# The last sixteen attention groups scored and valued in couples, with the scheduler's durations refitted

## The chip, the cores and the metric

The kernel runs on one core of a Trainium2 chip. The metric is the device time of one execution in microseconds (us); less is better. A profile is one execution recorded by the hardware. PE is TensorE's matmul side (PEld its weight loads, which run beside the multiplications), DVE is VectorE, ACT ScalarE, POOL GpSimd, and SP is SyncE, whose queue issues the DMAs.

## What is computed

A windowed attention over 8 batches x 8 heads x 576 positions x 64 numbers, and a feed-forward layer with a softplus behind it, all in fp32:

```python
scores = scale * np.matmul(q, k.transpose(0, 1, 3, 2))
mask_plain = (rel >= 0) & (rel < window)                     # window 32, heads 0 to 3
mask_dil = (rel >= 0) & (rel < window * dilation) & (rel % dilation == 0)   # dilation 4, heads 4 to 7
...
attn = np.exp(scores)
attn = attn / (np.sum(attn, axis=-1, keepdims=True) + 1e-09)
return np.matmul(attn, v)                                    # becomes x, 4608 x 512
...
h = x @ w_in                                                 # 512 x 2048
g = np.maximum(h, 0.0) + np.log1p(np.exp(-np.abs(h)))
return g @ w_out                                             # 2048 x 512
```

## The kernel before

**Tiles.** The 4608 tokens are 9 chunks of 512. Each chunk has 4 pairs of heads, so there are 36 groups of attention, numbered n = 4 x chunk + pair; pairs 0 and 1 are plain, 2 and 3 dilated. The feed-forward products work on 128 x 512 tiles; each fp32 operand is split into a high and a low part, so a product is three multiplications (a step of two tiles is six). The last six chunks are taken as three doubles of two chunks, each computed with seven products of blocks in place of eight. There are 3168 multiplications of 128 x 512 in the program, before and after the change. Positions in the program are given below by their count: "B 1296" is the place behind 1296 of them.

**A group of attention.** PE visits it twice. The scores visit (32 small multiplications into the PSUM tile `sv_ps`; the trace counts 64 records) multiplies `k` and `q`. Then DVE adds the mask (`maximum`, L441) and takes the maximum (L452), ACT does eight exponentials (L463), DVE sums, divides and turns 32 x 32 squares (L475 to L503). SP sends the squares to a DRAM tile `turned` (`send_squares`) and brings them back in four DMAs as `pt` (`fetch_squares`, the task "bring"). The values visit (32 small multiplications, 64 records) multiplies `pt` and `v`, and ACT copies the result into x (L589, `x_full`). `sv_ps` is two banks of PSUM. The scores of group n and the values of group n-1 share it: scores in the left half of each bank, values in the right (`HALF`). In order, then, PE scores n, values n-1, scores n+1, and so on; the two can be one visit ("jointly") or two.

**What sets the order.** PE, DVE, ACT and SP each run their queue in program order. The opening is written out by hand; from group 12 on (`double`) a planner inside the program writes all queues: a list scheduler that advances a clock, with a `Task` for each operation (engine, cost in us, what it waits for) and `choose(t)` for what PE does next. `visits` is the list of attention visits; a scores visit is taken when `t >= spaced` and, unless its time is urgent, when the values can join it (`joins`), else a product is taken. Multiplications pass through `matmul` (L238) and DMAs through `load_dma` (L173), so all of them have one line in the profile. The costs are numbers like these (`attention` and `values_of`):

```python
s = scored[n] = Task(f"scores {n}", PE, 1.06, lambda: score_of(n), deps)
v = valued[n] = Task(f"values {n}", PE, 1.30, lambda: value_of(n), deps)
together[scored[n]] = Task(f"both {n}", PE, 2.10, both)
```

The feed-forward work around the visits has PE write `h_x` and `h_y` (a block's product x @ w_in) and `o_ps` (g @ w_out); ACT and DVE combine them (L1424, L1426), compute the softplus (`e`, L1437 to L1447), and split g (L1467, L1471). SP streams the weights `t<-w_o`, `t<-w_two` and the like through rotating tiles.

Of the kernel before, what the change touches and what calls it, by code (L numbers as in the profile page):

```python
# [24 lines left out]
P = 128  # L25
# [44 lines left out]
MARGIN = 0.4  # L70
VISIT_EVERY = 8.0
NEG = -1.0e9
DEPTH = 4
# [43 lines left out]
def tile_windowed_attention_softplus_ffn(  # L117
# [35 lines left out]
    identb = consts[:, :P]  # L153
    ident = const.tile([P, P], F32, name="ident")
    slots, at = [], {0: 0, 1: 0, 2: 0}
# [144 lines left out]
    x_full, blocks = {}, {}  # L300

    def x_half(c, k):
        if (c, k) not in x_full:
            tag = "x_" + ("abcd" if c == FIRST else "cdab")[2 * ((c - FIRST - 1) % 2) * (c > FIRST) + k]
            x_full[c, k] = const.tile([P, 2, CH], F32, name="x_full", tag=tag)
        return x_full[c, k]
# [57 lines left out]
    class Group:  # L364
# [7 lines left out]
        def __init__(self, c, pr):  # L372
            self.c, self.pr, self.dil = c, pr, pr >= NPR // 2
            self.n, self.scaled_by, self.beside = c * NPR + pr, None, None
            self.own, self.masked = c == 0, c < 2
            self.places = PLACES[self.n] if self.n < len(PLACES) else "aaa"

        def load_k(self, engine=None):
            kw = DKW if self.dil else PKW
            self.k = scratch([P, kw], "k", self.c, self.pr)  # L380
            src = kdl[self.c, self.pr - 2] if self.dil else kpl[self.c, self.pr]
            load_dma(engine, out=self.k, in_=src)

        def load_q(self):
            self.q = scratch([P, CH], "q", self.c, self.pr)
            load_dma(out=self.q, in_=qp[self.c, self.pr])
# [5 lines left out]
        def load_v(self):  # L392
            self.v = scratch([P, NB, 2, D], "v", self.c, self.pr)
# [5 lines left out]
        def score(self, shared=None):  # L399

            self.banks, self.scored = shared or two_banks(
                "s_ps", {"a": None, "h": "hh", "o": ("o1", "o2")}[self.places[0]]
            )
            for t in range(NS):
                for g in range(NG):
                    for r in range(2):
                        rows = slice(r * D, (r + 1) * D)
                        q0, k0 = first_of(self.dil, t, g)
                        matmul(
                            out=self.banks[r][g * BLK : (g + 1) * BLK, t * WKEYS : (t + 1) * WKEYS],  # L410
                            lhsT=self.q[rows, q0 : q0 + BLK],
                            rhs=self.k[rows, k0 : k0 + WKEYS],
                            start=not self.masked or t == 0,
                            stop=not self.masked,
                        )
# [9 lines left out]
        def maximum(self):  # L425
            self.s = s = scratch([P, 2 * SW], "s", self.c, self.pr)
            self.blocks = s.rearrange("p (t k) -> p t k", k=WKEYS)
# [72 lines left out]
        def turn_squares(self):  # L500

            squares = const.tile([P, NG, NS, SQ], F32, name="squares", tag="q1")
            pin(nc.vector.transpose(  # L503
# [8 lines left out]
        def fetch_squares(self):  # L512
            self.pt = scratch([P, NG, NS * SQ], "pt", self.c, self.pr)
            for c in range(NG):
# [20 lines left out]

        def weighted(self, shared=None, following=None):

            banks, src = shared or two_banks("a_ps", ("o1", "o2") if self.places[2] == "o" else None)
            if shared:
                banks, src = [b[:, HALF:] for b in banks], [b[:, :, HALF:] for b in src]  # L540
# [44 lines left out]
        def x_high(self):  # L585
            if self.c >= FIRST:
                self.x = x_half(self.c, self.pr // 2)[:, self.pr % 2], None, self.src
            for dh, _, src in self.x_parts():
                copied = nc.scalar.copy(out=dh, in_=src)  # L589
                pin(copied)  # L590
                if self.c >= FIRST and self.n + 1 < len(groups):
# [334 lines left out]
    def value_of(n):  # L926

        if n + 1 < len(groups):
# [102 lines left out]
    class Ring:  # L1031
# [7 lines left out]
        def take(self, until):  # L1039
            self.holders = self.holders[1:] + [until]  # L1040

    class Task:

# [14 lines left out]
        def open(self, t):  # L1058
            return (
                self.after <= t + 1e-9  # L1060
                and all(
                    d.over(t + LATENCY * (getattr(d, "engine", PE) == self.engine != PE)) for d in self.deps
                )
# [40 lines left out]
    def run(task, t, engine=PE):  # L1104
# [111 lines left out]

    last_sum, last_more = [None], [None]

    def sums_of(i, p, deps):

        over = {}
        takes = lambda what: [(a_ring, Later(lambda: over.get(what)))]
        rank = 4.0
# [59 lines left out]

    def loads(n):
        if n >= len(groups):
            return
        g = groups[n]
        loaded[n, "q"] = Task(f"q {n}", SP, 0.256, g.load_q, [scored[n - 1]], rank=0.9)
        loaded[n, "k"] = Task(f"k {n}", SP, 0.32, g.load_k, [scored[n - 1]], rank=0.9)
        if g.pr == 0:  # L1290
            masks_in[g.c] = Task(f"mask {g.c}", SP, 0.128, lambda: load_mask(g.c), [scaled_of[n - 1]], rank=0.9)

    def values_of(n):

        deps = [brought.get(n), loaded.get((n, "v")), scaled_of.get(n + 1), x_done.get(n - 1)]
        v = valued[n] = Task(f"values {n}", PE, 1.30, lambda: value_of(n), deps)
        if n + 1 < len(groups):
            loaded[n + 1, "v"] = Task(f"v {n + 1}", SP, 0.512, groups[n + 1].load_v, [v], rank=1.0)
# [4 lines left out]
    def attention(n):  # L1303

        soon[0] = SOONER
        if n == len(groups):
            values_of(n - 1)
            return
# [7 lines left out]
        loads(n + 1)  # L1316
        values_of(n - 1)
        for t in range(NB):
            last = Task(
# [3 lines left out]
        last = Task(f"divide {n}", DVE, 0.70, lambda: g.divide(nc.vector), [last], rank=0.3)  # L1323
        last = turned_of[n] = Task(f"turn {n}", DVE, 0.71, g.turn_squares, [last, sent_squares.get(n - 1)], rank=0.3)
        last = sent_squares[n] = Task(f"send {n}", SP, 0.256, g.send_squares, [last], rank=0.1)
        brought[n] = Task(f"bring {n}", SP, 0.5, g.fetch_squares, [last, valued[n - 1]], rank=0.1)

# [202 lines left out]
    for d in range(DOUBLES):  # L1530
        for p in range(NPAIR):
            for k, (x, weights, role, begins, to, temp) in enumerate(steps):
# [55 lines left out]
                takes = [(e_ring, plus)]  # L1588
                one = Task(f"abs {name}", ACT, 1.16, lambda n=n, key=key: abs_of(n, key), [mine, unit_first[to], last_abs[0]], takes=takes)
                last_abs[0] = one  # L1590
                two = Task(f"exp {name}", ACT, 1.16, lambda key=key: late_exp(key), [one])
                plus.deps.append(Task(f"log {name}", ACT, 1.16, lambda key=key: late_log(key), [two]))
                if n == 1:
# [154 lines left out]

    for n in range(double, len(groups) + 1):
# [6 lines left out]
        if n % (2 * NPR) == NPR and n > double:  # L1756
            prepared((n - double) // (2 * NPR) - 1)

    visits = [part for n in range(double, len(groups)) for part in (scored[n], valued[n - 1])]
    visits.append(valued[len(groups) - 1])  # L1760
    scores = set(scored.values())
    together = {}
    for n in range(double, len(groups)):

# [3 lines left out]

        together[scored[n]] = Task(f"both {n}", PE, 2.10, both)
    spaced, done_second = HANDED_VISIT, 0  # L1770
# [30 lines left out]
    for n in brought:  # L1801
        users_of[brought[n]].append(scored.get(n + 1, valued[n]))
    latest = {}
# [47 lines left out]
    while first or second or visits or any(queues.values()):  # L1851
# [7 lines left out]
        if free_at[PE] <= t + 1e-9 and (queue := choose(t)) is not None:  # L1859
# [5 lines left out]
            else:  # L1865
                run(task, t)
            if task in scores:
                spaced = t + (VISIT_EVERY if len(visits) > 32 else LATE_VISITS)
            elif queue is second:
# [122 lines left out]
```

## Time and profile before

| | before |
|---|---|
| time, median of 3 runs | 831.25 us (829.7 to 832.61) |
| the profiled execution's own time | 833.33 us |
| its span, first to last instruction | 831.5 us |
| PE busy | 815.6 us, 98% of the span |
| DVE busy | 656.1 us, 79% |
| ACT busy | 577.7 us, 69% |
| mean granted clock of TensorE | 0.989 |

The profiled execution is 2.08 us above the median of the runs. A busy share is an average over stages; matmuls are pipelined, so that a busy PE is one with a multiplication under way, which is not to say that each takes its least time.

### The profile page before, as it was taken

The numbers are of one execution on the slowest core, as the hardware profiler recorded it, in microseconds if no ns is written. First come the engines' busy times: TensorE is split into PE (matmuls) and PEld (weight loads), VectorE is DVE, ScalarE is ACT, GpSimd is POOL, SyncE is SP. The second block draws the span as 40 slices with busy tenths as digits, with TensorE's granted clock in tenths as the row PEclk, the third lists the DMA queues.
The fourth block names the chain that finished last, engine by engine and source line by source line (L and its number), as shares of the span: only waits on it lengthen the run. The fifth ranks groups of instructions, "written<-read, shape, count | busy, mean of one in ns | idle before, by whom it ended". The sixth has DMA issues, their size and how long they took to land.

```text
span 831.5 us, 19565 instructions
## 1 busy us (share of the span) xinstructions
PE 815.6 (98%) x7841; PEld 662.6 (80%) x7841; DVE 656.1 (79%) x935; ACT 577.7 (69%) x1241; POOL 64.0 (8%) x74
## 2 busy tenths in 40 slices
PE   6899999999999999999999999999999999999997
PEld 3688888888888888788888888788878888888786
DVE  5798899957897798678889986778798957577964
ACT  6797778857676877578889546786796436776632
POOL 0000000031353360000000000000000000000000
PEclk7899999999999999999999999999999999999999
DMA  8788944468999887665777769897867576667662
GB/s 249 249 273 267 308 132 144 135 205 264 300 318 340 308 317 236 208 201 187 219 228 238 259 198 309 271 279 255 269 222 235 175 242 215 185 194 215 215 200 105
DMA packets 99947, 194.82 MB, mean 234 GB/s; under 512 B 10128, under 2 KB 43024, under 8 KB 99856
## 3 DMA queue, kind: packets, MB, share of 16 engines
q1 hardware_dynamic: 99712, 193.29, 72.1%
q8 instruction: 62, 1.02, 0.5%
q10 hardware_dynamic: 144, 0.28, 0.1%
q14 instruction: 29, 0.24, 0.1%
HBM read 145.29 MB, written 48.23 MB: 233 GB/s over the span
## 4 chain that ended last, share of the span: by engine, by line
PE 92%; DMA 4%; DVE 1%; ACT 1%; issue 0%; SPq 0%; ACTq 0%
PE o_ps L238 41%; PE h_ps L238 16%; PE h_x L238 14%; PE h_y L238 13%; PE sv_ps L238 6%; DMA q<-qp 1%; PE a_ps L238 1%; DMA t<-w_o 1%; DMA turned<-squares 1%; DMA raw<-w 1%; DMA consts<-cst 1%; PE s_ps L238 0%; PE t_ps L492 0%; DVE g L1471 0%; DMA k<-kpl 0%
## 5 line engine op out<-in xcount | busy, mean ns | idle before, releaser
L238 PE MATMUL o_ps<-g,t 128*128 128x512 f32 x864 | 209.6, 390 | 1.5 <-DMA t<-w_o 1.1
L238 PEld LDWEIGHTS o_ps<-g,t 128*128 128x128 f32 x864 | 161.3, 188 | 36.5 <-DMA t<-w_o 1.5
L238 PE MATMUL o_ps<-g,parts 128*128 128x512 f32 x576 | 142.1, 392 | 0.0
L238 PE MATMUL h_ps<-xh,parts 128*128 128x512 f32 x384 | 130.9, 397 | 0.0
L238 PEld LDWEIGHTS o_ps<-g,parts 128*128 128x128 f32 x576 | 107.1, 188 | 22.4
L1467 ACT CAST g<-stored 128x1024 fp32r<-128x1024 f32 x72 | 75.6, 1050 | 66.8 <-PE o_ps L238 64.9
L1471 DVE TENSOR_TENSOR g<-stored,g 128x1024 fp32r<-128x1024 f32 x72 | 87.8, 1221 | 32.4 <-ACT g L1467 32.2
L238 PEld LDWEIGHTS h_ps<-xh,parts 128*128 128x128 f32 x384 | 72.7, 189 | 15.5
L463 ACT ACTIVATE s<-s,nm 128x64 f32<-128x64 f32 x224 | 74.8, 337 | 12.1 <-DVE nm L452 11.7
L238 PE MATMUL h_ps<-xl,parts 128*128 128x512 f32 x192 | 75.3, 392 | 0.0
L238 PE MATMUL h_x<-s,t 128*128 128x512 f32 x276 | 70.6, 391 | 0.0
L238 PE MATMUL h_y<-s,t 128*128 128x512 f32 x276 | 70.6, 391 | 0.0
L799 POOL TENSOR_TENSOR a<-a 128x256 f32<-128x256 f32 x64 | 58.0, 914 | 99.8 <-DVE a L794 87.7
L1447 DVE SCALAR_TENSOR_TENSOR stored<-stored,e 128x1024 f32<-128x1024 f32 x48 | 58.4, 1219 | 4.4 <-ACT e L1443 4.4
L238 PEld LDWEIGHTS h_x<-s,t 128*128 128x128 f32 x276 | 51.5, 188 | 10.9
L238 PEld LDWEIGHTS h_y<-s,t 128*128 128x128 f32 x276 | 51.5, 188 | 10.8
L1462 DVE TENSOR_TENSOR stored<-stored 128x1024 f32<-128x1024 f32 x48 | 58.3, 1221 | 0.5
L1443 ACT ACTIVATE e<-e 128x1024 f32<-128x1024 f32 x48 | 50.8, 1060 | 1.1
L1440 ACT ACTIVATE e<-e 128x1024 f32<-128x1024 f32 x48 | 50.8, 1058 | 0.8
L1437 ACT ACTIVATE e<-stored 128x1024 f32<-128x1024 f32 x48 | 50.4, 1055 | 1.2 <-DVE stored L1426 0.7
L669 DVE SCALAR_TENSOR_TENSOR e<-h_ps,e 128x512 f32<-128x512 f32 x48 | 32.8, 683 | 21.7 <-ACT e L1147 16.9
L675 ACT CAST g<-e 128x512 fp32r<-128x512 f32 x48 | 29.5, 618 | 18.5 <-DVE e L669 9.6
(104 smaller groups left out, 1257.7 us busy)
## 6 DMA issues: line engine op xcount, KB each, us to landing
t<-w_o SPq DMA_DIRECT2D x84, 512.0 KB, 4.2
raw<-w SPq DMA_DIRECT2D x64, 256.0 KB, 4.3
v<-vp SPq DMA_DIRECT2D x28, 512.0 KB, 5.1
t<-w SPq DMA_DIRECT2D x20, 512.0 KB, 4.3
t<-w_two SPq DMA_DIRECT2D x20, 512.0 KB, 4.1
q<-qp SPq DMA_DIRECT2D x35, 256.0 KB, 3.9
w_o<-stage SPq DMA_DIRECT2D x32, 256.0 KB, 4.7
t<-w_one SPq DMA_DIRECT2D x16, 512.0 KB, 4.8
```

The source lines that it names most:

```text
L238: return tc.keep_in_program_order(nc.tensor.matmul(**kw))
L463: pin(nc.scalar.activation(out=self.blocks[:, t], in_=src, func=AF.Exp, bias=self.nm[:, t : t + 1], scale=1.0 / 8.0 if self.masked else 1. ...
L669: pin(nc.vector.scalar_tensor_tensor(out=e, in0=tiles.pop(i), scalar=0.0, in1=e, op0=ALU.max, op1=ALU.add))
L675: pin((copy or nc.scalar.copy)(out=gh, in_=ready[i]))
L799: pin(nc.gpsimd.tensor_tensor(out=out, in0=in0, in1=in1, op=ALU.subtract))
L1437: pin(nc.scalar.activation(out=es[key], in_=raw_g(*key), func=AF.Abs))
L1440: pin(nc.scalar.activation(out=es[key], in_=es[key], func=AF.Exp, scale=-1.0))
L1443: pin(nc.scalar.activation(out=es[key], in_=es[key], func=AF.Ln, bias=1.0))
L1447: pin(nc.vector.scalar_tensor_tensor(out=h, in0=h, scalar=0.0, in1=es.pop(key), op0=ALU.max, op1=ALU.add))
L1462: pin(nc.vector.tensor_tensor(out=raw_g(c, *PLACE[name]), in0=raw_g(c, *PLACE[a]), in1=raw_g(c, *PLACE[b]), op=op))
L1467: pin(nc.scalar.copy(out=set_of(k)[0], in_=raw_g(c, *PLACE[name])))
L1471: pin(nc.vector.tensor_tensor(out=low, in0=raw_g(c, *PLACE[name]), in1=high.bitcast(F32), op=ALU.subtract))
```

## The change

Groups 20 to 35 (`COUPLED = 20`) are taken two at a time. `scores_of_two` scores both groups of a couple in one visit (64 small multiplications), the first group in the left half of the two banks and the second, its "mate", in the right. `values_of_two` does the values of both in another visit, and one copy of 128 x 1024 (`x_of_two`) takes both to x in place of two of 128 x 512. The mate needs places of its own: its q lies where the squares lay, its k in two tiles (and so comes by two DMAs), its s and then pt in `a3`, its squares where s lay, and its v in the home of the x that will be written after it. The planner gets a gap of `COUPLE_EVERY` = 24 us between couples of scores, and shorter costs for scores, values, both, and the softplus steps on ACT, and an overlap of 0.10 us for operations that follow each other on DVE or ACT. The core of the diff:

```diff
+COUPLED = 20
+COUPLE_EVERY = 24.0
+COUPLE_SOONER = 28.0
...
+            self.mate = self.n >= COUPLED and pr % 2 == 1
...
+            if half:
+                self.banks = [b[:, HALF:] for b in self.banks]
+                self.scored = [b[:, :, HALF:] for b in self.scored]
...
+    def x_of_two(self):
+            c, k = self.c, self.pr // 2
+            pin(nc.scalar.copy(
+                out=x_half(c, k).rearrange("p k (h n) -> p k h n", h=2),
+                in_=self.src[0].rearrange("p h (k n) -> p k h n", k=2),
+            ))
...
+    def scores_of_two(n):
+        both = two_banks("sv_ps")
+        for j in range(2):
+            groups[n + j].score(both, j)
+
+    def values_of_two(n):
+        both = two_banks("sv_ps")
+        for j in range(2):
+            groups[n + j].weighted(both, None, j)
...
+    OVERLAP, EXP_OVERLAP = {"DVE": 0.10, "ACT": 0.10}, 0.01
...
-            free_at[task.engine] = t + cost
+            free_at[task.engine] = t + cost - overlap_of(task)
...
-        s = scored[n] = Task(f"scores {n}", PE, 1.06, lambda: score_of(n), deps)
+        s = scored[n] = Task(f"scores {n}", PE, 0.93, lambda: score_of(n), deps)
...
+    def attention_of_two(n):
+
+        soon[0] = COUPLE_SOONER
+        c = groups[n].c
+        s = scored[n] = Task(
+            f"scores {n}", PE, 1.58, lambda: scores_of_two(n),
+            [x_done[n - 1], *(loaded[n + j, name] for j in range(2) for name in "qk")],
+        )
...
+        v = valued[n] = valued[n + 1] = Task(
+            f"values {n}", PE, 2.13, lambda: values_of_two(n),
+            [*(brought[n + j] for j in range(2)), *(loaded[n + j, "v"] for j in range(2))],
+        )
+        x_done[n] = x_done[n + 1] = Task(
+            f"x {n}", ACT, 1.07, groups[n].x_of_two, [v, *x_uses.get(n // 2, [])], rank=0.3
+        )
...
-        elif visits and visits[0].open(t):
+        elif visits and visits[0].open(t) and (t >= spaced or visits[0] not in couples):
             return visits
...
+            if task in couples:
+                spaced = t + COUPLE_EVERY
```

From B 513 on, PE made 33 visits before: 16 joint ones, 8 of scores alone and 9 of values alone. Now it makes 25: 8 joint ones (up to scores of 19), one of values alone (group 19, at B 1116), 8 couples of scores (B 1122, 1242, 1344, 1452, 1560, 1818, 1956, 2088) and 8 couples of values (B 1224, 1332, 1440, 1548, 1806, 1944, 2076, 2214). Up to about B 432 the multiplications stand in the same order.

PE's queue before, around B 1296: the scores of group 24 (`sv_ps<-k,q`) and the values of group 23 (`sv_ps<-pt,v`) between products of a double.

```order
L238 MATMUL o_ps_4957<-g,t 128x512 x3
L238 MATMUL o_ps_4961<-g,t 128x512 x3
L238 MATMUL sv_ps<-k,q 32x64 x32
L238 MATMUL sv_ps<-pt,v 64x32 x32
L238 MATMUL h_x<-s_4391,t_3733 128x512
L238 MATMUL h_x<-s_4392,t_3733 128x512
```

PE's queue after the change, from B 1332: the values of groups 22 and 23, then the scores of 24 and 25.

```order
L241 MATMUL sv_ps<-pt,v 64x32 x64
L241 MATMUL h_y<-s_4461,parts 128x512
L241 MATMUL h_y<-s_4462,parts 128x512
L241 MATMUL h_y<-s_4461,parts 128x512 x2
L241 MATMUL h_y<-s_4462,parts 128x512
L241 MATMUL h_y<-s_4461,parts 128x512
L241 MATMUL h_x<-a_3930,parts 128x512
L241 MATMUL h_x<-a_3931,parts 128x512
L241 MATMUL h_x<-a_3930,parts 128x512 x2
L241 MATMUL h_x<-a_3931,parts 128x512
L241 MATMUL h_x<-a_3930,parts 128x512
L241 MATMUL sv_ps<-k,q 32x64 x64
```

A visit has become two of twice the size, with 12 multiplications between the values of one couple and the scores of the next, and 90 to 246 between a couple's scores and its values.

ACT's queue before, around group 22: eight exponentials in a row, and two copies of x.

```order
L463 ACTIVATE s,sm<-s,nm 128x64 x8
L1467 CAST g<-stored 128x1024
L1437 ACTIVATE e<-stored 128x1024
L1424 COPY stored<-h_x 128x512
L1437 ACTIVATE e<-stored 128x1024
L589 COPY x_full<-sv_ps 128x512
```

ACT's queue after the change, between the values of groups 20 and 21 and the exponentials of 22 and 23.

```order
L633 COPY x_full<-sv_ps 128x1024
L1546 ACTIVATE e<-e 128x1024
L1540 ACTIVATE e<-stored 128x1024
L1527 COPY temps<-h_x 128x512
L1543 ACTIVATE e<-e 128x1024
L1570 CAST g<-stored 128x1024
L1540 ACTIVATE e<-stored 128x1024
L497 ACTIVATE s,sm<-s,nm 128x64 x2
L1527 COPY stored<-h_x 128x512
L497 ACTIVATE s,sm<-s,nm 128x64 x14
```

Sixteen exponentials now stand together, with one other operation among them; in later couples more operations of the feed-forward stand among them.

SP's queue after the change, at the end of the softmax of a couple (before, one `turned<-squares` and four `pt<-turned` stood there for one group).

```order
L176 DMA turned<-squares 128x512 x2
L176 DMA t<-w_two 128x1024
L176 DMA pt<-turned 32x4x128 x8
L176 DMA t<-w_1474 128x512
L176 DMA q<-qp 128x512
```

The squares of both groups are sent, one weight load is between, and eight DMAs bring both back.

## Rows read from the trace of the kernel before

**Rows 1.** The page's engine line, and the chain that ended last by engine.

```profile
PE 815.6 (98%) x7841; PEld 662.6 (80%) x7841; DVE 656.1 (79%) x935; ACT 577.7 (69%) x1241; POOL 64.0 (8%) x74
...
PE 92%; DMA 4%; DVE 1%; ACT 1%; issue 0%; SPq 0%; ACTq 0%
```

**Rows 2.** Busy time by 20-us window, with granted clock, DMA share, GB/s.

```profile
520.00:540.00 20.00, 18.94 (x262) 15.04 (x261) 14.97 (x24) 14.27 (x43) 0.00 (x0) 1.00 0.85 277
```

**Rows 3.** PE's waits by releaser: us in total, times, longest.

```profile
PE s_ps L238 <- DMA k<-kpl: 2.8, 1, 2.8
...
PE o_ps L238 <- DMA t<-w_o: 1.1, 1, 1.1
PE sv_ps L238 <- DMA pt<-turned: 1.0, 2, 0.6
...
PE o_ps L238 <- DVE g L1471: 0.4, 1, 0.4
```

**Rows 4.** Timeline of PE, a joint visit: start, duration, operation.

```profile
570.78 1.52 PE L238 MATMUL h_x<-s,t 128*128 128x512 f32 x6
572.23 0.86 PE L238 MATMUL sv_ps<-k,q 64*32 64x64 f32 x64
573.02 1.13 PE L238 MATMUL sv_ps<-pt,v 64*64 64x32 f32 x64
574.09 1.66 PE L238 MATMUL h_y<-s,t 128*128 128x512 f32 x6
575.58 1.54 PE L238 MATMUL h_x<-a,t 128*128 128x512 f32 x6
```

**Rows 5.** Timeline of PE, a visit of scores alone.

```profile
331.80 1.52 PE L238 MATMUL o_ps<-g,parts 128*128 128x512 f32 x6
333.25 0.86 PE L238 MATMUL sv_ps<-k,q 64*32 64x64 f32 x64
...
335.54 0.62 PE L238 MATMUL h_x<-s,t 128*128 128x512 f32 x2
```

**Rows 6.** Timeline of PE, a visit of values alone.

```profile
544.15 1.52 PE L238 MATMUL h_y<-s,t 128*128 128x512 f32 x6
545.61 1.13 PE L238 MATMUL sv_ps<-pt,v 64*64 64x32 f32 x64
546.67 1.66 PE L238 MATMUL h_x<-a,t 128*128 128x512 f32 x6
548.17 1.52 PE L238 MATMUL h_y<-s,t 128*128 128x512 f32 x6
549.53 0.62 PE L238 MATMUL o_ps<-g,t 128*128 128x512 f32 x2
```

**Rows 7.** The tile sv_ps: duration in ns, min/median/max.

```profile
L238 PE MATMUL sv_ps<-k,q x1792: 212/216/240, 94.0 to 609.7; 64*32 64x64 f32 x200
...
L589 ACT COPY x_full<-sv_ps x28: 564/581/622, 123.4 to 636.7; 128x512 f32<-128x512 f32 x28
```

**Rows 8.** Timeline of group 22, from its scores to its values.

```profile
343.72 0.86 PE L238 MATMUL sv_ps<-k,q 64*32 64x64 f32 x64
...
346.74 0.35 ACT L463 ACTIVATE s<-s,nm 128x64 f32<-128x64 f32 x1
...
347.08 0.34 ACT L463 ACTIVATE s<-s,nm 128x64 f32<-128x64 f32 x1
...
352.42 0.88 SPq L173 DMA_DIRECT2D turned<-squares  x1
...
355.90 1.75 SPq L173 DMA_DIRECT2D pt<-turned  x4
...
360.76 0.95 PE L238 MATMUL sv_ps<-pt,v 64*64 64x32 f32 x51
```

**Rows 9.** The tile turned: DMA from issue to landing, both kinds.

```profile
DMA to landing us min/median/max: 1.8/3.0/5.8
```

**Rows 10.** Timeline of ACT in the exponentials of group 24.

```profile
378.53 1.06 ACT L1437 ACTIVATE e<-stored 128x1024 f32<-128x1024 f32 x1
...
381.68 0.33 ACT L463 ACTIVATE s<-s,nm 128x64 f32<-128x64 f32 x1
```

More of the change, by code (lines that the diff above doesn't have):

```diff
@@ L376, in __init__, with keys_at @@
             self.places = PLACES[self.n] if self.n < len(PLACES) else "aaa"
+            self.mate = self.n >= COUPLED and pr % 2 == 1
         def load_k(self, engine=None):
             kw = DKW if self.dil else PKW
+            src = kdl[self.c, self.pr - 2] if self.dil else kpl[self.c, self.pr]
+            if self.mate:
+                last = kw - kw % CH if kw < DKW else 3 * (PER + WIN)
+                ends = slice(0, last), slice(3 * (PER + WIN), kw)
+                self.k = [
+                    (at, const.tile([P, at.stop - at.start], F32, name="k", tag=tag))
+                    for at, tag in zip(ends, ("a2", "ident"))
+                ]
+                for at, part in self.k:
+                    load_dma(out=part, in_=src[:, at])
+                return
             self.k = scratch([P, kw], "k", self.c, self.pr)
-            src = kdl[self.c, self.pr - 2] if self.dil else kpl[self.c, self.pr]
             load_dma(engine, out=self.k, in_=src)
+        def keys_at(self, rows, k0):
+            if not self.mate:
+                return self.k[rows, k0 : k0 + WKEYS]
+            at, part = next((at, part) for at, part in self.k if at.start <= k0 and k0 + WKEYS <= at.stop)
+            return part[rows, k0 - at.start : k0 - at.start + WKEYS]
         def load_q(self):
-            self.q = scratch([P, CH], "q", self.c, self.pr)
+            if self.mate:
+                self.q = const.tile([P, CH], F32, name="q", tag="q1")
+            else:
+                self.q = scratch([P, CH], "q", self.c, self.pr)
             load_dma(out=self.q, in_=qp[self.c, self.pr])
@@ L392, in load_v @@
         def load_v(self):
-            self.v = scratch([P, NB, 2, D], "v", self.c, self.pr)
+            if self.mate:
+                self.v = const.tile([P, NB, 2, D], F32, name="v", tag=home_of_x(self.c, self.pr // 2))
+            else:
+                self.v = scratch([P, NB, 2, D], "v", self.c, self.pr)
             if self.masked:
@@ L425, in maximum @@
         def maximum(self):
-            self.s = s = scratch([P, 2 * SW], "s", self.c, self.pr)
+            if self.mate:
+                self.s = s = const.tile([P, 2 * SW], F32, name="s", tag="a3")
+            else:
+                self.s = s = scratch([P, 2 * SW], "s", self.c, self.pr)
             self.blocks = s.rearrange("p (t k) -> p t k", k=WKEYS)
@@ L500, in turn_squares @@
         def turn_squares(self):
-            squares = const.tile([P, NG, NS, SQ], F32, name="squares", tag="q1")
+            squares = const.tile([P, NG, NS, SQ], F32, name="squares", tag="s" if self.mate else "q1")
             pin(nc.vector.transpose(
@@ L512, in fetch_squares @@
         def fetch_squares(self):
-            self.pt = scratch([P, NG, NS * SQ], "pt", self.c, self.pr)
+            if self.mate:
+                self.pt = const.tile([P, NG, NS * SQ], F32, name="pt", tag="a3")
+            else:
+                self.pt = scratch([P, NG, NS * SQ], "pt", self.c, self.pr)
             for c in range(NG):
@@ L1040, in take, with overlap_of @@
             self.holders = self.holders[1:] + [until]
+    def overlap_of(task):
+        if not isinstance(task, Task):
+            return 0.0
+        return EXP_OVERLAP if task.name.startswith("exps") else OVERLAP.get(task.engine, 0.0)
     class Task:
@@ L1317, in attention, with softened_scores @@
         values_of(n - 1)
+        softened_scores(n, last, [valued[n - 1]])
+    def softened_scores(n, last, unread):
+        g = groups[n]
         for t in range(NB):
@@ L1747, in tile_windowed_attention_softplus_ffn @@
         tag_freed(key, done)
-    for n in range(double, len(groups) + 1):
+    last_sums = [task for over in overs for task in over.values()]
+    for n in range(double, COUPLED):
         attention(n)
@@ L1755, in tile_windowed_attention_softplus_ffn @@
                 x_uses[2 * (FIRST + 2) + k] = [split_done[k], staged_free[STAGED - 1]]
-        if n % (2 * NPR) == NPR and n > double:
-            prepared((n - double) // (2 * NPR) - 1)
-    visits = [part for n in range(double, len(groups)) for part in (scored[n], valued[n - 1])]
-    visits.append(valued[len(groups) - 1])
-    scores = set(scored.values())
+    values_of(COUPLED - 1)
+    visits = [part for n in range(double, COUPLED) for part in (scored[n], valued[n - 1])]
+    visits.append(valued[COUPLED - 1])
+    scores = set(scored.values())
+    for n in range(COUPLED, len(groups) + 1, 2):
+        if n % (2 * NPR) == NPR:
+            prepared((n - double) // (2 * NPR) - 1)
+        if n == len(groups):
+            break
+        if n == COUPLED:
+            loads_of_mate(n + 1, scored[n - 1])
+        attention_of_two(n)
+        visits += [scored[n], valued[n]]
+        soon[0] = 0.0
+    couples = {scored[n] for n in range(COUPLED, len(groups), 2)}
     together = {}
-    for n in range(double, len(groups)):
+    for n in range(double, COUPLED):
         def both(n=n):
```

82 lines of the change are left out of this document (52 added, 30 removed).

## The prediction, made before the result was known

> **What bounds the kernel.** I read the page first: PE is busy 98% of the span, and 92% of the chain that ended last is PE's [rows 1]. DVE and ACT have a quarter of their time free. So a change counts only by what it takes from PE's queue, or by a wait that it puts into it. Then the waits: the largest, 2.8 us, stands in the opening on the tile `s_ps`, which the change doesn't touch. In the planned stretch PE waits once 1.1 us for weights of the second product (`t<-w_o`), twice for squares brought back (1.0 us together) and 0.4 us for DVE's g [rows 3]: 2.5 us, all that could be won there. The window that holds the 1.1 us shows PE short of 20 us by just that, with the full clock (1.00) granted [rows 2]. What is left is what a visit costs PE beyond its multiplications, and that is read from three places of the timeline.
>
> The unit is one 128 x 512 multiplication in a row of its like: 548.17 to 549.53 for six, 0.2267 us each [rows 6].
>
> - Scores alone: 331.80 to 335.54 is 3.74 us and holds 12 of them (2.72), so the visit costs 1.02 us [rows 5].
> - Values alone: 544.15 to 548.17 is 4.02 us for 12 of them, so 1.30 us [rows 6].
> - Jointly: 570.78 to 575.58 is 4.80 us for 12 of them, so 2.08 us [rows 4].
>
> Inside a visit, 64 records of scores take 0.86 us, of which the last one's own duration is 0.22 [rows 4, 7]: 0.64 us are the work of a group, and 0.91 in the values (1.13 less 0.22). The rest is a fixed price: 0.38 us for scores alone, 0.39 for values alone, 0.53 for a joint visit.
>
> **The change, part by part.** *Fewer visits.* A couple has one fixed price and the work of two: scores 0.38 + 2 x 0.64 = 1.66 us, values 0.39 + 2 x 0.91 = 2.21 us. From B 513 on there were 16 joint, 8 scores alone and 9 values alone: 33.3 + 8.2 + 11.7 = 53.2 us. Now there are 8 joint, 1 of values alone, 8 couples of each: 16.6 + 1.3 + 13.3 + 17.7 = 48.9 us. That saves **4.3 us**. The ends: if the eight visits less are worth only a single visit's fixed price each, 8 x 0.38 = 3.0 us; if each of the 16 couples pays another 0.18 us at its middle (a third of a joint visit's 0.53, which has three changes of tile size where a single visit has two), 4.3 - 2.9 = 1.4 us. No couple is in the trace of before, so the middle is not seen. But within one group the 64 records go over both banks and all quarters of the array at an even pace [rows 4], and the second half of a couple is more of the same; so I take no price at its middle. [...]
>
> *One copy of x in place of two.* Two copies cost ACT 2 x 0.58 us [rows 7]; one of 128 x 1024 should be about 1.06, as other 1024-wide operations [rows 10]. PE needs the banks back before the next couple of scores, 12 multiplications later, 2.7 us. Copies often come late behind other operations, but the planner places this one with the scores waiting on it. Nothing to PE; up to about 1 us for each of the seven such places if ACT is caught in a chain of three (378.53 to 381.68 [rows 10]).
>
> *A longer chain from scores to values.* This is the part that can cost. For group 22 the scores ended at 344.58 and the values began, without a wait for squares, at 360.76 [rows 8]: 16.2 us at most for mask, maximum, exponentials, divide, turn, the send (3.5 us from issue to the next issue) and the bring (1.75 us of issuing). A couple adds a second mask operation (0.7 us), eight more exponentials at 0.34 us (346.74 to 347.08 [rows 8]), 2.7 us, and four more DMAs, 1.75 us: 21.3 us. The room between a couple's scores and its values is 90 to 102 multiplications for groups 20 to 27, and 90 x 0.2267 is 20.4 us, with 0.3 us at both edges; the mate's squares are needed only halfway through the visit, 0.9 us later: 21.6 us. So it just fits. For groups 28 to 35, with 120 to 246 multiplications (27 us and more), it fits with 6 us over. Against it speaks group 24 before, where three feed-forward steps stood among its exponentials and took 3.15 us [rows 10]; but in the new queue of ACT the exponentials of 20, 21, 26 and 27 stand without a break and those of 22 and 23 with one copy among them. Landings spread from 1.8 to 5.8 us [rows 9], and one late landing of 5.8 where 3.0 was the middle is 2.8 us. I take 1.5 us of waits at the four close couples, with ends 0 and 12 us (2.9 at each, worked out below). Behind a waiting values visit stand the multiplications of `h_y` and `h_x`; ACT and DVE go on meanwhile, so nothing else comes late by it.
>
> *More DMAs and other homes.* Each of eight mates issues its k by two DMAs, 8 issues more on SP in 300 us at about 0.44 us (four take 1.75 [rows 8]): SP has the room, but the weight loads behind them start that much later. The one that waited before (1.1 us [rows 3]) had 18 multiplications between the freeing of its tile and its use; in the new queues the shortest such distance among the couples is 24. I take 0.5 us in place of 1.1, with ends 0 and 2.5.
>
> *Refitted costs.* They issue nothing themselves. They move products and feed-forward steps, and the planner's softplus and overlap come closer to the rows (three chained steps in 3.15 us, 1.05 each [rows 10], entered at 1.16 before and 1.07 less 0.10 of overlap now). What is hidden is hidden by the queue's lead over PE; where the new costs are too short, PE meets an operation not done. I take 0.5 us of such waits, as before (0.4 [rows 3]), ends 0 and 3.
>
> *Sum.* Waits 2.5 us before against 1.5 + 0.5 + 0.5 = 2.5 after: nothing. Visits -4.3, within 3.0 to 4.3; I take -4.2. The profiled execution took 833.33 us in all, which becomes **829.1**; it lies 2.08 us above the median, so against 831.25 I forecast **827.0 us**.
>
> **The rivals.**
>
> - *Values wait for their squares (the opposite side).* Place: PE at the values of couples 20, 22, 24 and 26. With the three feed-forward steps among its exponentials that group 24 had, 3.15 us [rows 10], a couple needs 21.3 + 3.15 = 24.5 us where there are 21.6: 2.9 us late at each, 12 us in all. 831.25 - 4.2 + 12 - 1.0 (the waits for squares before) = 838. From (2.5 + 4.2 + 1.0) / 4, about 1.9 us at each, it is slower by over 0.3%. For it: a late step among the exponentials of either group delays both, and values already wait for squares now [rows 3]. Against it: the unbroken exponentials.
> - *The gain is given back in part.* A wait of some 0.7 to 1.5 us at three or four places (squares, x copied late before the next scores, products whose feed-forward step isn't done): 2 to 5 us, so 829 to 832, within 0.3%.
> - *A price at the middle of a couple*, as if it were a visit's change: saving 1.4, so 829.9, within 0.3%.
> - *The waits go too.* The waits for squares were two [rows 3], the later couples have 27 us, and the weights more distance: 2.5 us less than before, so 824.5.
> - *The change is only a shift*: visits saved, but the multiplications next to the couples run slower, so that PE is as busy as before: 831. Little speaks for it, since the fixed price is seen at the edges only [rows 4 to 6].
>
> **How the numbers follow.** About 0.3%, 2.5 us here, is what a measurement can tell from no change. The forecast (825.5 to 828.7) gets 0.56, the waits going too 0.09: faster 0.65. Given back 0.20, a price at the middle 0.06, a mere shift 0.03: same 0.29. Values waiting by more than 1.9 us each: slower 0.06. The range from 824.0 to 831.0 leaves out some 0.03 below, 0.07 of the given-back cases and the 0.06 above.
>
> **What would show it right or wrong.** In the profile of the changed kernel: a couple of scores costs 1.6 to 1.7 us beyond the multiplications around it, a couple of values 2.2, with an even pace through 128 records; the ACT copy 128 x 1024 takes about 1.05 us and no scores visit waits for it; PE's waits name `pt<-turned` for at most 1.5 us in all and `t<-w_o` for about 0.5; PE's busy time falls by about 4 us. The prediction is wrong if `pt<-turned` or the copy of x show several us before values or scores of groups 20 to 27, if a step of 0.1 us or more stands between records 64 and 65 of a couple, or if new waits on ACT's or DVE's feed-forward steps appear where the refit moved products closer.

## The result, and the profile after

The changed kernel takes 839.05 us (median of 6 runs, 837.38 to 839.46), the kernel before in 6 runs 833.29 us (829.7 to 835.11): ratio 1.0067, 95% interval 1.0045 to 1.0089. It is slower by 0.7%; 827.0 was forecast.

The page of the changed kernel, engine line and chain by engine:

```profile
PE 815.8 (97%) x7839; PEld 659.2 (79%) x7841; DVE 649.2 (78%) x935; ACT 574.1 (69%) x1233; POOL 64.6 (8%) x74
...
PE 84%; DVE 7%; DMA 5%; ACT 3%; issue 1%; SPq 0%; DVEq 0%; ACTq 0%
```

Against [rows 1], PE's share of the chain fell from 92% to 84%; DVE's rose from 1% to 7%, ACT's from 1% to 3%, DMA's from 4% to 5%, and 1% is "issue" (a wait without a releaser in the profile). PE's busy time is 815.8 us and has not fallen. PE's waits, the ones in the planned part:

```profile
PE o_ps L241 <- DVE g L1574: 1.8, 5, 0.4
PE sv_ps L241 <- issue: 1.7, 2, 1.2
...
PE h_y L241 <- DVE stored L1529: 0.8, 1, 0.8
PE o_ps L241 <- DMA t<-w_o: 0.6, 1, 0.6
PE h_y L241 <- DVE a L1529: 0.6, 1, 0.6
```

In [rows 3] there were 2.5 us of such waits, mostly for DMAs. None of the new ones is for squares (`pt<-turned`), and none for the copy of x. The couples themselves are as forecast; a couple of values and the next couple of scores on PE's timeline:

```profile
349.09 1.52 PE L241 MATMUL h_y<-s,t 128*128 128x512 f32 x6
350.54 2.07 PE L241 MATMUL sv_ps<-pt,v 64*64 64x32 f32 x128
352.54 1.66 PE L241 MATMUL h_x<-a,parts 128*128 128x512 f32 x6
354.04 1.52 PE L241 MATMUL h_y<-s,parts 128*128 128x512 f32 x6
355.40 1.52 PE L241 MATMUL h_x<-a,parts 128*128 128x512 f32 x6
356.85 1.48 PE L241 MATMUL sv_ps<-k,q 64*32 64x64 f32 x128
358.26 1.67 PE L241 MATMUL h_y<-s,t 128*128 128x512 f32 x6
359.77 1.55 PE L241 MATMUL h_x<-a,parts 128*128 128x512 f32 x6
```

Values: 349.09 to 354.04 is 4.95 us with 12 multiplications (2.72): 2.23 us, forecast 2.21. Scores: 355.40 to 359.77 is 4.37 us with 12 of them: 1.65 us, forecast 1.66.

**Where the time went.** The opening does not take the same time in every profile: the 463rd multiplication of 128 x 512 (B 462) begins between 154.3 and 158.9 us in the profiles below, with PE waiting there for its first loads by differing amounts. So I compared the traces multiplication by multiplication, from B 462 to the last. The time between the starts of two successive ones is 0.2267 us at best; what lies above it is PE's loss, and it falls into four kinds: intervals that hold a visit (less the pauses inside it), pauses inside visits, other intervals over by more than 0.03 us (waits; for these "the end" is from B 2376 on, after the last visit), and the sum of smaller excesses (pace). In us, from one profile of each kernel (those of the experiments below are here too):

| kernel | visits | pauses in visits | waits | waits at the end | pace | sum |
|---|---|---|---|---|---|---|
| before | 52.7 | 1.3 | 1.4 | 0.8 | 1.3 | 57.5 |
| changed kernel | 48.6 | 2.6 | 3.0 | 4.4 | 4.5 | 63.1 |
| refit_alone | 51.7 | 3.3 | 8.5 | 6.0 | 1.9 | 71.5 |
| couples_old_costs | 48.7 | 2.2 | 6.5 | 0.7 | 4.0 | 62.1 |
| apart | 48.5 | 2.1 | 4.9 | 4.3 | 4.3 | 64.2 |
| after_ident_first | 48.6 | 3.0 | 3.1 | 4.4 | 1.5 | 60.5 |
| before_ident160 | 52.6 | 0.1 | 1.1 | 0.8 | 4.2 | 58.9 |
| after_no_overlap | 48.5 | 3.8 | 10.5 | 0.2 | 4.2 | 67.1 |
| after_dependent_whole | 49.2 | 2.3 | 7.5 | 2.8 | 4.1 | 65.9 |
| old_costs_first | 48.7 | 2.1 | 5.7 | 0.8 | 1.1 | 58.5 |
| old_costs_first_apart | 49.0 | 2.4 | 4.6 | 0.8 | 1.3 | 58.1 |
| old_costs_first_apart9 | 48.7 | 0.8 | 11.9 | 0.8 | 1.3 | 63.6 |
| first_overlap_till_last_visit | 48.6 | 3.5 | 2.1 | 0.4 | 1.3 | 55.9 |
| old_costs_first_apart_margin | 48.6 | 0.3 | 11.3 | 0.8 | 1.1 | 62.0 |
| first_till_last_apart_margin | 48.4 | 0.0 | 11.3 | 0.3 | 1.6 | 61.5 |

From before to the changed kernel: visits -4.1, pauses +1.3, waits +1.6, waits at the end +3.6, pace +3.2: +5.6 us, where the medians differ by 5.8. Three losses were to be explained: the pauses, the waits at the end and the pace. The 1.6 us of other waits are taken up again below.

**Pauses inside couples of scores.** There are four, 0.35, 0.75, 1.37 and 0.11 us, with no releaser. The longest:

```profile
541.21 0.81 PE L241 MATMUL sv_ps<-k,q 64*32 64x64 f32 x59
543.18 0.92 PE L241 MATMUL sv_ps<-k,q 64*32 64x64 f32 x69 [1.17 <-issue]
544.03 0.50 PE L241 MATMUL h_x<-s,t 128*128 128x512 f32 x1
```

**Waits at the end.** PE falls short in four of the windows from 700 to 800 us, where before it was busy but for 0.45 us at 760 to 780 (last row). Columns: window, its length, PE, PEld, DVE, ACT and POOL busy, granted clock, DMA share, GB/s.

```profile
700.00:720.00 20.00, 19.44 (x86) 15.45 (x84) 13.62 (x17) 9.94 (x12) 0.00 (x0) 1.00 0.67 220
740.00:760.00 20.00, 19.38 (x85) 15.38 (x84) 15.18 (x18) 12.42 (x14) 0.00 (x0) 1.00 0.61 179
760.00:780.00 20.00, 19.23 (x82) 14.91 (x81) 13.76 (x16) 18.35 (x20) 0.00 (x0) 1.00 0.66 211
780.00:800.00 20.00, 19.56 (x85) 15.68 (x84) 17.22 (x16) 8.33 (x9) 0.00 (x0) 1.00 0.62 206
```

```profile
760.00:780.00 20.00, 19.55 (x86) 15.74 (x85) 15.79 (x16) 17.99 (x19) 0.00 (x0) 1.00 0.65 201
```

**Pace.** Of the multiplications at the end, 280 of some 790 took over 0.228 us, 21 before, although PE never stopped between them. It shows in a stretch without a wait, here 786.52 to 792.03, 5.51 us for 24 of them, where 24 x 0.2267 is 5.44:

```profile
786.52 5.67 PE L241 MATMUL o_ps<-g,t 128*128 128x512 f32 x24
792.03 2.90 PE L241 MATMUL o_ps<-s,t 128*128 128x512 f32 x12
794.77 5.67 PE L241 MATMUL o_ps<-g,t 128*128 128x512 f32 x24
```

By the program's addresses, 176 of the 198 multiplications at the end that take g from two particular tiles were slow (0.2324 us in the mean of the 198), and 102 of 577 others. Of these 102, 69 stand among the six multiplications next behind one of the 198, so that the slowness reaches a little beyond them; why is not shown. Of the rest 33 in 449 were slow. Those two tiles lie ahead of `ident` in memory. The change enlarges `ident` from 128 to 160 columns, and with that all tiles behind it lie 128 bytes further: before, all operands of these multiplications began at 128 bytes past a multiple of 256; now the two tiles of g still do, and the rest, weights among them, begin at a multiple of 256.

### The profile page after: what moved, and what is told of

It reads as the page before. It is cut to its first block, busy times and chain, and to the rows that moved or that the text cites. A ratio compares the mean times of both kernels' runs of the same rounds, so it can differ in the third digit from the quotient of the medians.

```text
span 837.2 us, 19572 instructions
## 1 busy us (share of the span) xinstructions
PE 815.8 (97%) x7839; PEld 659.2 (79%) x7841; DVE 649.2 (78%) x935; ACT 574.1 (69%) x1233; POOL 64.6 (8%) x74
## 3 DMA queue, kind: packets, MB, share of 16 engines
q8 instruction: 62, 1.02, 0.5%
## 4 chain that ended last, share of the span: by engine, by line
PE 84%; DVE 7%; DMA 5%; ACT 3%; issue 1%; SPq 0%; DVEq 0%; ACTq 0%
PE o_ps L241 39%; PE h_ps L241 15%; PE h_y L241 12%; PE h_x L241 12%; PE sv_ps L241 5%; DVE g L1574 1%; DVE stored L1550 1%; DMA raw<-w 1%; DVE stored L1565 1%; DMA q<-qp 1%; ACT e L1540 1%; DMA v<-vp 1%; ACT e L1543 1%; ACT g L1570 1%; DMA k<-kpl 1%
## 5 line engine op out<-in xcount | busy, mean ns | idle before, releaser
L241 PE MATMUL o_ps<-g,t 128*128 128x512 f32 x864 | 213.2, 393 | 2.5 <-DVE g L1574 1.8
L241 PEld LDWEIGHTS h_x<-s,t 128*128 128x128 f32 x276 | 51.4, 188 | 11.9 <-DVE stored L1529 0.6
L1565 DVE TENSOR_TENSOR stored<-stored 128x1024 f32<-128x1024 f32 x48 | 58.5, 1221 | 0.7
```

The costliest lines, as they stand in the source:

```text
L241: return tc.keep_in_program_order(nc.tensor.matmul(**kw))
L1565: pin(nc.vector.tensor_tensor(out=raw_g(c, *PLACE[name]), in0=raw_g(c, *PLACE[a]), in1=raw_g(c, *PLACE[b]), op=op))
```

## The experiments

Ratios are to runs of the kernel before on the same chip, with their 95% intervals.

**Costs and couples apart.** couples_old_costs keeps the couples and puts back the planner's costs:

```diff
-    OVERLAP, EXP_OVERLAP = {"DVE": 0.10, "ACT": 0.10}, 0.01
+    OVERLAP, EXP_OVERLAP = {"DVE": 0.0, "ACT": 0.0}, 0.0
...
-        s = scored[n] = Task(f"scores {n}", PE, 0.93, lambda: score_of(n), deps)
+        s = scored[n] = Task(f"scores {n}", PE, 1.06, lambda: score_of(n), deps)
```

In the same way values go from 1.20 to 1.30, both from 1.99 to 2.10, and each softplus step on ACT from 1.07 to 1.16.

> The couples with the planner's old costs for scores, values, both, the softplus steps, and no overlap. Theory A (the refitted costs make the planner give PE products before ACT and DVE are done): the waits of the last 790 multiplications fall from about 3 us to under 1 us, the visits keep their 4 us, the pauses inside the couples of scores stay (2 to 3 us), so the ratio to before is 0.996 to 1.000. Theory B (the couples themselves crowd ACT, DVE and SP): the waits of the tail stay, ratio 1.004 or more.

Measured 1.0056 (1.0032 to 1.0080). The waits at the end are gone (4.4 to 0.7 us), as theory A has it, but not the time: 6.5 us are lost between the visits, and pauses without a releaser, between and inside visits, come to 5.1 us.

refit_alone does the reverse, the kernel before with the new costs and the overlap:

> The kernel before with the refitted costs and the overlap, without couples. Theory A: slower than before, ratio 1.004 to 1.008, with waits for DVE's g, a and stored in the last 790 multiplications of 2 to 4 us and no pause inside a visit of scores. Theory B: ratio 0.998 to 1.002 and waits as before.

Measured 1.0160 (1.0134 to 1.0186), slower than either theory said. Its waits at the end are 6.0 us without a single couple, so they are the refit's. From 300 us on PE's waits are:

```profile
PE o_ps L238 <- DVE g L1478: 4.2, 6, 1.4
PE sv_ps L238 <- issue: 2.1, 1, 2.1
PE o_ps L238 <- DMA t<-w_o: 1.4, 2, 0.9
PE h_y L238 <- DVE a L1433: 1.3, 2, 0.7
```

I had expected no pause inside a visit here; there is one of 2.1 us.

**Pauses.** The kernel apart holds a couple's scores back after a couple's values:

```diff
             if task in couples:
                 spaced = t + COUPLE_EVERY
+            elif task in values_coupled:
+                spaced = max(spaced, t + 6.5)
```

> The changed kernel with 24 or more multiplications, in place of 12, between a couple's values and the next couple's scores. Theory C (the pauses inside the couples of scores, 2.6 us in four of them, come from PE's code: two blocks of 256 instructions are used up within 5 us, and the block loaded last comes too late): the pauses fall to under 0.3 us in all, and the time by 2 to 3 us against the changed kernel, ratio to before 1.003 to 1.005. Theory D (the second half waits for the mate's q or k): the pauses stay, 2 us or more.

Measured 1.0098 (1.0070 to 1.0125): no gain. The pauses without a releaser fell from 2.6 to 1.1 us, all in one couple, but values now waited for their squares (1.1 us inside visits), and PE elsewhere (4.9 in place of 3.0 us). On the pauses theory C holds, and not by this run alone: counted over all instructions of PE's queue (multiplications, weight loads, and the semaphore instructions between them), every pause of over half a microsecond that the profile puts down to "issue" behind the opening, in every kernel here, stands at instruction 191 of a block of 256, counted from 0 (11711 and 12479 in the changed kernel, three times 256 apart; the pause of 0.11 us stands at 13247, that of 0.35 us at 10687). I call this place the edge of a block. The page shows the loads:

```profile
q8 instruction: 62, 1.02, 0.5%
```

The 62 packets are 16 KB each, and PE's queue has 15,908 instructions, 15,680 of them multiplications and weight loads: some 256 instructions a packet. One packet lies just before the pause above, in the window 540.8 to 541.9:

```profile
q1 hardware_dynamic: 118, 0.44, 98.8%
q8 instruction: 1, 0.02, 5.3%
```

It began at 540.94, 3.6 us after PE had passed the last edge of a block (537.30, in the values of the couple before), and landed at 541.88; PE went on at 543.18, 1.3 us later. Of the seven places where a couple of scores follows one of values, the four with a pause had their load begin 2.3 to 3.6 us after the edge before it, and the next edge came 4.4 to 4.6 us behind that edge; in the three without a pause it began 1.1 and 1.9 us after it, and once 2.4, with the next edge 5.8 us behind (18 multiplications stand between the visits there, not 12). A couple of values, 12 multiplications and a couple of scores are 536 instructions in some 6.5 us, where 256 instructions of large multiplications take 28 us. What makes the load begin so late is not shown; in the window above the DMA engines were 98.8% busy with other transfers (q1).

**Places of tiles.** after_ident_first is the changed kernel with `ident` reserved ahead of all tiles, which moves all of them alike, so that all operands of the multiplications at the end begin at a multiple of 256; before_ident160 is the kernel before with the larger `ident` alone:

```diff
+    ident = const.tile([P, DKW // 4], F32, name="ident", tag="ident")[:, :P]
     a_tiles = [const.tile([P, DM], F32, name="a", tag=f"a{k}") for k in range(5)]
...
-    ident = const.tile([P, DKW // 4], F32, name="ident", tag="ident")[:, :P]
```

```diff
-    ident = const.tile([P, P], F32, name="ident")
+    ident = const.tile([P, 160], F32, name="ident")[:, :P]
```

> The changed kernel with the enlarged tile ident reserved ahead of all other tiles, so that all tiles lie 128 bytes further, none only in part. Theory E (the enlarged ident moved all later tiles by 128 bytes against the two tiles of g that lie ahead of it, and multiplications that take g from those two run at 0.2325 us in place of 0.2267): these multiplications are back at 0.2267, 2.2 to 2.6 us are won between the first couple and the end, ratio to before 1.002 to 1.005. Theory F (they follow late operations closely, and their place in memory means nothing): no change, 1.006 to 1.008.

> The kernel before with the tile ident enlarged from 128 to 160 columns and nothing else. Theory E: multiplications that take g from the two lower tiles at about 0.2325 us, 2 to 2.5 us more, ratio 1.002 to 1.003. Theory F: no such multiplications, ratio 0.999 to 1.001.

Measured 1.0033 (1.0015 to 1.0051) and 1.0013 (0.9996 to 1.0031). The pace went from 4.5 to 1.5 us by the first and from 1.3 to 4.2 us by the second, 3 us either way and more than I had expected; the same instructions in the same order. The stretch shown above, in after_ident_first (783.69 to 789.13 is 5.44 us):

```profile
783.69 5.60 PE L241 MATMUL o_ps<-g,t 128*128 128x512 f32 x24
789.13 2.88 PE L241 MATMUL o_ps<-s,t 128*128 128x512 f32 x12
```

and in before_ident160 (5.51 us):

```profile
781.45 5.67 PE L238 MATMUL o_ps<-g,t 128*128 128x512 f32 x24
786.96 2.90 PE L238 MATMUL o_ps<-s,t 128*128 128x512 f32 x12
```

The interval of before_ident160's ratio alone would not settle it; the pace in its trace does. (Its sum is only 1.4 us above before's because this profile happens to lack 1.5 us of pauses and waits that the one of before has, most of them for DMAs.)

**Which part of the refit.** after_no_overlap keeps the new costs and sets the overlap to zero; after_dependent_whole lets only independent operations overlap. The edit of the second:

```diff
-                    d.over(t + (LATENCY + overlap_of(d)) * (getattr(d, "engine", PE) == self.engine != PE))
+                    d.over(t + LATENCY * (getattr(d, "engine", PE) == self.engine != PE))
```

> The changed kernel with the planner's overlap set to zero, all refitted costs kept. Theory A1 (it is the overlap, which lets a dependent operation begin 0.10 us before the one ahead ends, that makes plans too early): losses of over 0.03 us each in the last 790 multiplications fall from 4.4 us to 1.5 us or less, ratio to before 1.001 to 1.004. Theory A2 (it is the shorter costs of the softplus steps on ACT): the losses stay above 3 us.

> The changed kernel in which an operation that needs the one ahead of it on its own engine waits for its whole cost, and only independent ones overlap by 0.10 us. Theory A1: losses in the last 790 multiplications fall from 4.4 us to 2 us or less, ratio to before 1.001 to 1.005. Theory A2: they stay above 3 us.

Measured 1.0112 (1.0077 to 1.0146) and 1.0090 (1.0067 to 1.0113). Waits at the end: 0.2 and 2.8 us. So it is the overlap, and it is more than its use on dependent operations, for which 2 us or less was expected. But both plans lose 7 to 10 us between the visits, and part of that is TensorE's clock. In after_no_overlap a pause of 2.2 us at the edge of a block, and behind it:

```profile
530.20 0.50 PE L241 MATMUL h_y<-s,t 128*128 128x512 f32 x1 [2.23 <-issue]
530.53 2.20 PE L241 MATMUL o_ps<-g,t 128*128 128x512 f32 x6
532.54 2.51 PE L241 MATMUL h_x<-a,t 128*128 128x512 f32 x6
```

```profile
531.00:535.00 4.00, 4.00 (x12) 3.12 (x11) 3.96 (x5) 1.39 (x3) 0.00 (x0) 0.57 0.89 269
```

Eight multiplications there ran at 0.427 us in place of 0.2267, and the granted clock over the 4 us was 0.57. The pause cost 2.4 us itself and 1.6 us behind it. In after_dependent_whole fourteen multiplications took 6.12 us at a granted clock of 0.50:

```profile
337.50:344.00 6.50, 6.12 (x14) 4.79 (x15) 4.99 (x7) 4.35 (x19) 0.00 (x0) 0.50 0.45 162
```

In all, the granted clock fell six times behind the opening: twice in after_no_overlap and once each in after_dependent_whole, refit_alone, old_costs_first_apart9 and old_costs_first_apart_margin (the last two are below). It cost 3.0 us in after_dependent_whole and 1.3 to 1.8 us each time elsewhere, and stands in the column of waits. Ahead of a fall PE had stood idle once for 2.1 or 2.2 us, or two or three times close together for 1.8 to 3.7 us in all. Idle times of 1.17 us in the changed kernel and 1.81 us in couples_old_costs were not followed by a fall.

**Together.** Three kernels with the old costs and `ident` first, without and with the spacing (6.5 and 9.0 us):

> Couples with the planner's old costs, and ident reserved ahead of all other tiles. Theory E: the multiplications after the first couple are all near 0.2267 us, 2.5 to 3 us less than the run couples_old_costs, ratio to before 1.001 to 1.003. If the places of tiles mattered only together with the refit, nothing changes (1.005).

> The same with at least 24 multiplications between the values of a couple and the next scores. Theory C (pauses come from PE's code, where two or three blocks of 256 instructions are used up in a few us): the pauses without a releaser, 5.0 us in couples_old_costs, fall to 1.5 us or less, ratio to before 0.997 to 1.000. Rival: another wait takes their place, as in the run apart, ratio 1.001 or more.

> The same with at least 36 multiplications there, and so 60 to 102 between scores and values of most couples. Theory C: no pause without a releaser over 0.3 us. The chain from scores to values, 21 us by the prediction, is longer than the shortest of these rooms (60 multiplications, 14 us): values wait for their squares 1 us or more at the last couple, ratio 0.999 to 1.004.

Measured 1.0025 (1.0004 to 1.0045), 1.0037 (1.0016 to 1.0058) and 1.0074 (1.0054 to 1.0094). The places are worth their 3 us with either plan (pace 1.1). The spacing takes the pauses at edges of blocks from 4.6 us to 0.7, and the rival is right about the rest; this is where the time went in old_costs_first_apart:

```profile
547.80 0.81 PE L241 MATMUL sv_ps<-pt,v 64*64 64x32 f32 x40
549.09 1.12 PE L241 MATMUL sv_ps<-pt,v 64*64 64x32 f32 x60 [0.48 <-DMA pt<-turned]
550.14 1.65 PE L241 MATMUL h_x<-a,t 128*128 128x512 f32 x6
551.63 0.39 PE L241 MATMUL h_y<-s,t 128*128 128x512 f32 x1
552.58 0.61 PE L241 MATMUL h_y<-s,t 128*128 128x512 f32 x2 [0.56 <-issue]
```

Values wait in their middle for the squares, and the next edge of a block still pauses. With 9.0 us a pause of 1.3 us stayed, where theory C had none over 0.3; values waited 0.3 us for squares in place of 1 us or more; and PE lost 11.9 us between visits, in waits for g above all, and 1.6 us of it by the clock. So what I expected of this kernel failed in each part.

The last three put the findings together: the overlap used only while visits are left, then the spacing with a later start for values (1 us behind the landing of the squares), with the old costs, and with both. The edit of the first, beside `ident` first:

```diff
-        if not isinstance(task, Task):
+        if not isinstance(task, Task) or not visits:
             return 0.0
```

> The changed kernel with ident reserved first, and the planner's overlap used only while visits are left; the work behind the last visit is planned without it. Theory A1 (the overlap makes the end of the plan too early): losses of over 0.03 us in the last 790 multiplications fall from 4.4 us to under 1.5 us, the rest stays as in after_ident_first, so 3 us less than that run, ratio to before 0.999 to 1.001. Rival: the waits of the end come from what the couples leave behind, 4 us or more stay, ratio 1.003.

> As old_costs_first_apart, with couples entered at 1.66 and 2.25 us and a couple's values planned 1 us behind the landing of their squares. If the waits of values for squares (1.5 to 2.3 us there) are only a matter of the plan's margin, they vanish and nothing takes their place: ratio to before 0.997 to 1.000. If the couples need the time (PE waits elsewhere for g or stored then): 1.001 to 1.004.

> The first kernel of this batch with both spacings of the second. If pauses (2.6 to 3 us), the waits at the end (4.4 us) and the places of the tiles (3 us) are separate losses, what is left is the 4 us of fewer visits: ratio to before 0.995 to 0.999. If each wait that goes brings another, 1.000 to 1.004.

Measured 0.9972 (0.9953 to 0.9990), 1.0077 (1.0047 to 1.0108) and 1.0059 (1.0038 to 1.0080). The first did better than expected and is faster than both kernels: 830.36 us (12 runs) against 832.19 in the same comparison. Its waits at the end are 0.4 us, and PE's waits from 160 us on are two rows:

```profile
PE sv_ps L241 <- issue: 2.7, 4, 1.5
PE h_y L241 <- DVE stored L1529: 0.8, 1, 0.8
```

So the waits at the end and the places of the tiles are separate losses, and each could be taken away alone. The pauses are not: in both kernels with the spacing and the later start they vanish almost (0 to 0.3 us in visits), and the waits between visits grow to 11.3 us, so that both are slower than either side of their expectations; these waits are named by g and in the last kernel once by `t<-w_o`. The last kernel's rows:

```profile
PE o_ps L241 <- DVE g L1574: 3.8, 3, 1.8
PE o_ps L241 <- DMA t<-w_o: 1.7, 1, 1.7
```

## Why the prediction was wrong

- **Fewer visits: right.** -4.2 us was taken, -4.1 measured. There is no step at the middle of a couple: where nothing pauses, its 128 records of scores take 1.48 us, of values 2.07, and the 65th begins at most 0.04 us after the 64th. One reading behind the forecast was wrong without harm: the pace inside a group is not even (33 of the 64 records of scores begin in the first 0.27 us of 0.64). PE's busy time did not fall by the 4 us forecast, since the slower pace, which counts as busy, gave 3.2 us back.
- **One copy of x: right.** It takes 1.0 us, and no scores waited for it.
- **The longer chain from scores to values: right for the changed kernel, near its limit.** 1.5 us of waits were taken, none came. The rival of the opposite side named 838 us, near the 839.05 measured, but by luck: its place, values waiting for squares, cost nothing here. In kernels with less room (old_costs_first_apart) values do wait, 1.5 us in all by the table of waits.
- **"More DMAs and other homes" failed.** I costed only the extra DMA issues (0.5 us; `t<-w_o` cost 0.6) and looked at no home's address: the term was right for the DMAs and missing for the places. The larger `ident` cost 3.2 us of pace, in multiplications that the change doesn't touch, from the first couple to the end. That the place is the cause is shown by both directions, in after_ident_first and before_ident160; which part of the chip slows is not.
- **"Refitted costs" failed.** I took 0.5 us with ends 0 and 3; waits rose by 3.6 us at the end of the program alone, where there is no couple, and the runs put that on the overlap (0.2 us without it, 0.4 with it used only while visits are left). The sign that the prediction gave for being wrong came with it: new waits for DVE's g, stored and a. My reading that the new numbers came closer to the rows was wrong in one way that could be read from them: the old entries, 1.06, 1.30 and 2.10 for scores, values and both, are nearer to 1.02, 1.30 and 2.08 than 0.93, 1.20 and 1.99, and three chained steps on ACT took 3.15 us [rows 10], where the overlap plans them 0.97 apart.
- **A cost that had no term: PE's code.** A visit twice as long close behind another brings two edges of 256-instruction blocks close together: 4.4 to 4.6 us apart at the four pauses, where PE went on 1.2 to 1.6 us after a load had landed. That is 2.6 us of pauses in the changed kernel, where the kernel before has none at an edge beyond the opening.
- **What stays open.** Why the plans differ so much between the visits (1.1 to 11.9 us of waits) is not explained beyond the pauses at edges and the lower clock (1.3 to 3.4 us in five kernels), and neither are the 1.6 us that the changed kernel has more than the one before: any edit of the planner moves hundreds of operations, and the runs compare whole plans there. A version without pauses and without new waits was not found.

## What to carry to other kernels

A kernel at 98% PE is tuned as a whole: an edit that saves a sure 4 us there must be charged with all that it moves, the addresses of untouched tiles (3.2 us here) and the density of the instruction stream (2.6 us) included. Split the difference of two traces into kinds, multiplication by multiplication, before naming a cause; here the page's list of waits in the planned part grew by 3.0 us (2.5 to 5.5), where pauses, waits and pace together grew by 9.7. Planning too early cost 3.6 us at the end of the program, but taking the overlap away everywhere cost more between the visits (10.5 us of waits against 3.0), so neither way of erring is safe: the best kernel here used the overlap for one stretch and not for the other.

## What the runs showed of the hardware that was not expected

- At the end of the program, fp32 multiplications of 128 x 512 took 0.2269 us in the mean (before) and 0.2270 (after_ident_first) where the moving tile (the operand of 512 columns) and the weights begin at the same place within 256 bytes, both at 128 or both at 0, and 0.2324 (changed kernel) where the moving tile is at 128 and the weights at 0. All tiles behind `ident` lie as the weights do there, so it is not shown that the weights are what matters. The other mixed case was not run.
- The pages show 62 loads of PE's code of 16 KB each, before and after the change, and PE's queue (15,908 instructions in the changed kernel) has 62 of the edges named above, 256 instructions apart. In the couples' stretch of the changed kernel (324 to 620 us) a load began between some 4 us before PE passed the edge before it and 3.6 us after, and took 0.9 to 1.6 us. Where PE paused there at an edge with no releaser in the profile, it went on 1.2 to 1.6 us after a load's landing.
- In after_no_overlap an idle time of 2.2 us in an otherwise busy PE was followed by eight multiplications at 0.427 us in place of 0.2267 (granted clock 0.57); idle times of 1.17 us (changed kernel) and 1.81 us (couples_old_costs) were not followed by slow ones, but two of 1.0 and 0.8 us, one soon after the other in after_no_overlap, were.
